# Preparing most weight tiles beside the first pair of blocks instead of beside the attention

## The chip, the cores and the metric

The kernel runs on one core of one Trainium2 chip. The metric is the device time of one execution in microseconds (us), given as the median of several runs. A core has TensorE (PE in the profile, with its weight loads as PEld), VectorE (DVE), ScalarE (ACT), GpSimd (POOL) and SyncE (SP), which here issues most of the DMAs.

## The reference

Attention inside chunks of 64 tokens, then two feed-forward layers: one with a squared ReLU (d_ff 2048) and one gated by SiLU (d_ff 1536). All of it is in float32.

```python
def _attn_ref(q, k, v):                      # q, k, v: (8, 8, 576, 64)
    scores = scale * np.matmul(q_c, k_c.transpose(0, 1, 2, 4, 3))   # chunks of 64 tokens
    scores = scores - np.max(scores, axis=-1, keepdims=True)
    attn = np.exp(scores)
    attn = attn / (np.sum(attn, axis=-1, keepdims=True) + 1e-09)
    out = np.matmul(attn, v_c)
...
def _moe_ref(x, w_in, w_out):                # x: 4608 x 512, w_in: 512 x 2048
    h = np.maximum(x @ w_in, 0.0)
    return (h * h @ w_out).astype(np.float32)
...
def _moe2_ref(x, w_gate, w_val, w_out):      # d_ff 1536
    g = x @ w_gate
    silu = g * (1.0 / (1.0 + np.exp(-g)))
    val = x @ w_val
    return (silu * val @ w_out).astype(np.float32)
```

## The kernel before

**Blocks and sets.** The 4608 tokens are nine blocks of 512. They are worked on in five sets: block 0 alone, then four pairs. Attention goes by units of 256 tokens, two in a block; `EARLY` is 6, so the opening has the units of blocks 0, 1 and 2, and the units of each later set are worked on beside the set before it.

**Products in parts.** Each matmul operand is split into a high part (`high`, ACT, L154) and a low part (`low`, DVE, L157), and a product is three matmuls of 128x512 (`three`, L464 to L466). For a pair of blocks a job (`Pair`) needs seven products of six matmuls, after a scheme that saves an eighth of the products; its seven operands are sums and differences of the blocks (`Operands.sums`, `make`). For block 0 a job (`Single`) has four such products, 24 matmuls. There is one job for each pair of f tiles and each set: `n1` is 8, the pairs are `keys1`. A job (n, m) is that of set n and pair m. Its methods `p15`, `p6`, `p27` are run in its own turn, while `p4` and `p3` are run in the turn of the job behind it (`Products.run`, `late`). `p15` copies the running sum `px` out on ACT (`kept`) between product 1 and product 6, `p6` does so before product 7.

**The preparation.** `prep_pair` makes the weight tile W of one pair of f tiles in seven steps: load of two raw tiles of 64-bit words (512 KB each), `decode1` (ACT, L129 and L130), `decode2` (DVE, then two additions on GpSimd, L139), `decode3` (DVE, L144) with the first casts, the first lows with four sums on DVE, the cast of the sums, and the last low, after which W is stored to DRAM where the pair is a moving one. Pairs 0, 3 and 6 stay in SBUF; the others (`moving1`) are stored and loaded again for each later set (`load_combo`, L230; `ask` starts the load two uses ahead).

**The opening.** It is one loop (L758), in which PE, ACT, DVE and GpSimd keep the order in which the code is written (`ordered`). SyncE's order is set by a planner. In iteration i unit i has its scores (`attn_products`, `attn_less_max`, `attn_exp`, `attn_normed`), unit i-1 is turned, and unit i-2 has its values and goes out; three steps of preparation i and three of preparation i-1 stand between them. From iteration 4 on the jobs of block 0 are given, three at once and then one in each iteration; job 7 follows after the first job of the first pair. The sums of the pair are made in iteration 8.

**The stages behind.** From L1020 on only PE keeps the written order; the other engines' orders are the planner's. A job of a pair has four quarters, at each of which `beside1` puts other work: the attention of the next set, its sums, its operands.

**Memory.** Tiles of 4 KB a partition (raws, m, s, q, k, v, e, p, z, x, all operands, g) share 31 buffers of the tag `big`. W has five buffers (`wp`). The scores and the values of the later units share one PSUM tile (`banks2`, tag `a`, one buffer); six banks (`psb`) serve the rest. A tile gets its buffer at its first write, in the order of the code, and gives it back when all that read it are done.

Of the kernel before, what the change touches and what calls it, by code (L numbers as in the profile page):

```python
# [28 lines left out]
def attention_mlp_mlp_kernel(  # L29
# [29 lines left out]
    nc = tc.nc  # L59
# [9 lines left out]
    upb = BLOCK // UNIT  # L69
# [12 lines left out]
    ident = const.tile([P, P], F32, name="ident")  # L82

    def duo(name, dtype=F32):
        return big.tile([P, 2, BLOCK], dtype, tag="big", name=name)
# [40 lines left out]
    def decode1(raws, m):  # L126

        for t, raw in enumerate(raws):
            nc.scalar.activation(out=m[:, t, :], in_=word(raw, 1, F32), func=AF.Abs)  # L129
            nc.scalar.activation(out=word(raw, 0, I32), in_=word(raw, 0, U32), func=AF.Copy, scale=2.0**-29)  # L130

    def decode2(raws, m):
        mi = m.bitcast(I32)
        nc.vector.tensor_scalar(out=m, in0=m, scalar1=LEAST, scalar2=MOST, op0=ALU.max, op1=ALU.min)
        nc.vector.tensor_scalar(
            out=mi, in0=mi, scalar1=5, scalar2=2, op0=ALU.logical_shift_left, op1=ALU.logical_shift_right
        )
        for t, raw in enumerate(raws):
            nc.gpsimd.tensor_tensor(out=mi[:, t, :], in0=mi[:, t, :], in1=word(raw, 0, I32), op=ALU.add)  # L139

    def decode3(raws, m):
        mi = m.bitcast(I32)
        for t, raw in enumerate(raws):
            nc.vector.scalar_tensor_tensor(  # L144
                out=mi[:, t, :],
                in0=word(raw, 1, I32),
                scalar=TOP,
                in1=mi[:, t, :],
                op0=ALU.bitwise_and,
                op1=ALU.bitwise_or,  # L150
            )

    def high(src, hi):
        nc.scalar.copy(out=hi, in_=src)  # L154
# [25 lines left out]
    combos = {}  # L180
    wdram = {}

    def new_combo():
        return wp.tile([P, 2, 7, half], F32R, tag="W", name="W")
# [7 lines left out]
    def prep_pair(key, raws, keep, store):  # L192

        pair = raws.take(2)
        yield
        m = duo("m")
        decode1(pair, m)
        yield
        decode2(pair, m)
        yield  # L200
        decode3(pair, m)
        w = new_combo()
        a1, a22 = m[:, 0, :].rearrange("p (i c) -> p i c", i=2), m[:, 1, half:]
        high(a1, w[:, 0, 0:2, :])
        high(a22, w[:, 0, 2, :])
        yield
        low(a1, w[:, 0, 0:2, :], w[:, 1, 0:2, :])
        low(a22, w[:, 0, 2, :], w[:, 1, 2, :])
        s = big.tile([P, 4, half], F32, tag="big", name="s")
        a11, a12, a21 = m[:, 0, :half], m[:, 0, half:], m[:, 1, :half]  # L210
        s1, s2, s3, s4 = (s[:, i, :] for i in range(4))
        tt = nc.vector.tensor_tensor
        tt(out=s1, in0=a21, in1=a22, op=ALU.add)
        tt(out=s2, in0=s1, in1=a11, op=ALU.subtract)
        tt(out=s3, in0=a11, in1=a21, op=ALU.subtract)
        tt(out=s4, in0=a12, in1=s2, op=ALU.subtract)
        yield
        high(s, w[:, 0, 3:7, :])
        yield
        low(s, w[:, 0, 3:7, :], w[:, 1, 3:7, :])  # L220
        if store:
            wdram[key] = combo_dram(key)
            nc.sync.dma_start(out=wdram[key], in_=flat(w))
        if keep:
            combos[key] = w
        yield
# [171 lines left out]
    def attn_turned(u):  # L398
        ts, pt = at[u], duo("p")
        for j in range(2):  # L400
            for c in range(2):
                part = slice(c * CH, (c + 1) * CH)
                nc.scalar.copy(out=pt[part, j, :], in_=ts[j ^ c][part, :])
        at[u] = pt
# [252 lines left out]
    work = Work()  # L657
    n1 = nf1 // 2

    keys1 = [("i", fp) for fp in range(n1)]  # L660
    keys2 = [(name, fp) for fp in range(n2) for name in "gv"]
    moving1 = set(keys1) - set(keys1[::3])
# [3 lines left out]
    def raws_of(keys, ahead):  # L666
        return Raws([sources[name][2 * fp + t] for name, fp in keys for t in range(2)], ahead)
# [56 lines left out]
            self.late()  # L724


    make_identity(nc, ident)
    raws1 = raws_of(keys1, 0)
    preps = [prep_pair(key, raws1, True, key in moving1) for key in keys1]
    up1 = Products(keys1, moving1, 2, 1, lambda key: squared)  # L730

    def x_sums(n):
        up1.ops[n] = Operands()
        up1.ops[n].sums([xraw.pop(b) for b in sets[n]])

    early = list(range(EARLY))
    ready = {"x": upb + 2, "pair": len(early) + 2}

    def prepare(f, steps=1):
        if 0 <= f < n1:
            for _ in range(steps):
                next(preps[f])

    def loads(i):
        if i < len(early):
            attn_qk(early[i])
        prepare(i)
        if 1 <= i <= len(early):  # L750
            attn_v(early[i - 1])

    with ordered(ET.PE, ET.Activation, ET.DVE, ET.Pool):
        make_identity(nc, ident)
        loads(0)
        loads(1)
        given = 0
        for i in range(n1 + 1):  # L758
            loads(i + 2)
            unit = early[i] if i < len(early) else None  # L760
            turned = early[i - 1] if 0 <= i - 1 < len(early) else None
            valued1 = early[i - 2] if 0 <= i - 2 < len(early) else None
            if unit is not None:
                attn_products(unit)
            if turned is not None:
                attn_turn_pe(turned)
            if valued1 is not None:
                attn_values(valued1)
            prepare(i)
            prepare(i - 1)  # L770
            if i == ready["x"]:
                x_sums(0)
                up1.ops[0].make(1, 2, 4)
            prepare(i - 1)
            if i == ready["pair"]:
                x_sums(1)
                up1.ops[1].make(1, 5)
            if turned is not None:
                attn_turned(turned)
            prepare(i)  # L780
            if unit is not None:
                attn_less_max(unit)
                attn_exp(unit)
            prepare(i - 1)
            if i == ready["pair"]:
                up1.ops[1].make(6, 2, 7)
            if unit is not None:
                attn_normed(unit)
            if valued1 is not None:
                attn_out(valued1)  # L790
            if i >= ready["x"]:
                while given < min(n1, i - 1):
                    up1.run(0, given)
                    given += 1
            prepare(i)

    class Down:

# [182 lines left out]
    def attention_step(n, t):  # L981

        if n < len(sets):
            units = [b * upb + x for b in sets[n] for x in range(upb)]
            for what in ("out", "turn", "scores", "qk"):
                for u, when in zip(units, WHEN[what]):
                    if when == t:
                        if what == "out":
                            attn_values(u)
                            attn_out(u)  # L990
                        elif what == "turn":
                            attn_v(u)
                            attn_turn(u)
                        elif what == "scores":
                            attn_scores(u)
                        else:
                            attn_qk(u)

    def beside1(n, m):
        def at_quarter(i):  # L1000
            t = 4 * m + i
            attention_step(n + 1, t)
            attention_step(n + 2, t - LAST)
            if n + 1 < len(sets):
                if t == 24:
                    x_sums(n + 1)
                if t - LAST in OPS:
                    up1.ops[n + 1].make(*OPS[t - LAST])
            else:
                if t % 2 == 0:  # L1010
                    work.step(1)
                if t == LAST - 8:
                    down1.begin()
                if t == LAST - 4:
                    down1.split(0)

        return at_quarter

    attention_step(2, -3)
    with ordered(ET.PE):  # L1020
        for n in range(1, len(sets)):
            if n + 1 == len(sets):
                raws = Raws(w_out, 2)
                for f in range(nf1):
                    work.add(prep_plain("o", f, raws))
            for m in range(n1):
                up1.run(n, m, beside1(n, m))
                if n == 1 and m == 0:
                    up1.run(0, n1 - 1)
        up1.finish()  # L1030
    combos.clear()

# [158 lines left out]
```

## Time and profile before

| | us |
|---|---|
| median of 3 runs | 1702.23 |
| lowest, highest | 1698.13, 1702.32 |
| the profiled execution, its own time | 1701.53 |
| its span in the trace | 1699.8 |
| PE busy | 1612.9 |
| DVE busy | 1023.0 |
| ACT busy | 817.4 |

The profile is of one execution. Its span goes from the first to the last instruction, and the execution's own time is 1.7 us longer. An engine's busy time leaves out waits and the issue of DMAs. Where a row tells what ended an idle time, the name behind the arrow is that of the instruction or the DMA that was waited for. The clock is the granted share of TensorE's full clock, 2.4 GHz.

### The profile page before, as it was taken

To read this page: it belongs to the slowest core of one execution; us is meant where nothing else is said; L and a number is where in the kernel's file an instruction comes from. 1 tells how busy PE (TensorE), PEld (TensorE's weight loads), DVE (VectorE), ACT (ScalarE), POOL (GpSimd) and SP (SyncE) were. 2 spreads that over 40 slices of the span, in tenths; PEclk is the share of its full clock that TensorE was granted. 3 is DMA by queue.
4 is the path that set the end of the run, shared out by engine and by line. 5 is a ranking of instruction groups with operands and counts; after the bars stand their busy time and mean duration, and the time that the engine had idled before them with its cause. 6 is when DMAs were issued, how large, how long until landed. Compare 5 with 4: busy or idle time off the path is not lost.

```text
span 1699.8 us, 23601 instructions
## 1 busy us (share of the span) xinstructions
PE 1612.9 (95%) x9408; PEld 1324.9 (78%) x9408; DVE 1023.0 (60%) x1268; ACT 817.4 (48%) x1165; POOL 130.9 (8%) x94
## 2 busy tenths in 40 slices
PE   3868999999999999999999999999998999999997
PEld 3756777778888888888888788788787788788886
DVE  7884464655467656562312646547448796787884
ACT  5774676768775444442212434334335553434441
POOL 3220001010122111110000000000000120000000
PEclk8888999999999999999999999999999999999999
DMA  8555887887976668784309685567568999563342
GB/s 335 211 217 209 278 282 260 289 282 257 349 240 247 246 250 292 283 305 133 116 37 369 230 297 204 198 242 244 192 250 297 343 377 409 200 198 111 105 144 50
DMA packets 140367, 407.10 MB, mean 240 GB/s; under 512 B 47840, under 2 KB 57056, under 8 KB 128736
## 3 DMA queue, kind: packets, MB, share of 16 engines
q1 hardware_dynamic: 129888, 367.83, 61.2%
q10 hardware_dynamic: 10368, 37.75, 5.8%
q8 instruction: 74, 1.21, 0.3%
q14 instruction: 37, 0.30, 0.1%
HBM read 278.92 MB, written 123.47 MB: 237 GB/s over the span
## 4 chain that ended last, share of the span: by engine, by line
PE 82%; DMA 6%; DVE 6%; ACT 2%; issue 2%; SPq 1%; POOL 1%; DVEq 0%; ACTq 0%; POOLq 0%
PE px L464 10%; PE px L466 10%; PE px L465 9%; PE acc L464 6%; PE acc L466 6%; PE acc L465 6%; PE py L464 5%; PE pz L466 5%; PE py L465 5%; PE py L466 5%; PE pz L465 5%; PE pz L464 5%; DMA k<-in_k_dram 4%; PE accs L464 2%; PE accs L466 2%; PE accs L465 2%
## 5 line engine op out<-in xcount | busy, mean ns | idle before, releaser
L464 PE MATMUL px<-hi,W 128*128 128x512 f32 x640 | 252.3, 394 | 9.0 <-ACT hi L154 5.5
L466 PE MATMUL px<-lo,W 128*128 128x512 f32 x640 | 250.4, 391 | 3.6 <-DVE lo L157 3.6
L465 PE MATMUL px<-hi,W 128*128 128x512 f32 x640 | 249.9, 391 | 0.0
L139 POOL TENSOR_TENSOR m<-m,raw 128x512 int32<-128x512 int32 x68 | 94.0, 1399 | 1005.4 <-ACT u L532 565.1
L532 ACT COPY u<-px 128x512 f32<-128x512 f32 x160 | 92.5, 578 | 150.4 <-PE px L466 150.3
L464 PE MATMUL acc<-hi,w 128*128 128x512 f32 x416 | 161.8, 389 | 0.0
L465 PE MATMUL acc<-hi,w 128*128 128x512 f32 x416 | 161.8, 389 | 0.0
L466 PE MATMUL acc<-lo,w 128*128 128x512 f32 x416 | 161.5, 389 | 0.0
L464 PEld LDWEIGHTS px<-hi,W 128*128 128x128 f32 x640 | 120.7, 189 | 38.1 <-ACT hi L154 6.3
L518 DVE TENSOR_TENSOR g<-pz,u 128x512 f32<-128x512 f32 x112 | 76.9, 687 | 115.3 <-PE pz L466 74.9
L466 PEld LDWEIGHTS px<-lo,W 128*128 128x128 f32 x640 | 120.7, 189 | 29.8 <-DVE lo L157 4.4
L633 DVE TENSOR_TENSOR g<-g,sig 128x1024 f32<-128x1024 f32 x54 | 65.9, 1220 | 125.7 <-ACT sig L632 125.6
L157 DVE TENSOR_TENSOR lo<-graw,hi 128x1024 fp32r<-128x1024 f32 x72 | 91.4, 1269 | 82.7 <-PE acc L465 42.8
L465 PEld LDWEIGHTS px<-hi,W 128*128 128x128 f32 x640 | 120.7, 189 | 24.4
L154 ACT CAST hi<-h 128x1024 fp32r<-128x1024 f32 x93 | 95.4, 1053 | 92.0 <-DVE h L885 21.9
L464 PE MATMUL pz<-hi,W 128*128 128x512 f32 x320 | 126.3, 395 | 8.3 <-ACT hi L154 8.3
L466 PE MATMUL pz<-lo,W 128*128 128x512 f32 x320 | 126.5, 395 | 3.1 <-DVE lo L157 3.1
L464 PE MATMUL py<-hi,W 128*128 128x512 f32 x320 | 128.1, 400 | 0.0
L465 PE MATMUL pz<-hi,W 128*128 128x512 f32 x320 | 126.1, 394 | 0.0
L465 PE MATMUL py<-hi,W 128*128 128x512 f32 x320 | 125.9, 394 | 0.0
L466 PE MATMUL py<-lo,W 128*128 128x512 f32 x320 | 125.9, 393 | 0.0
L157 DVE TENSOR_TENSOR lo<-h,hi 128x1024 fp32r<-128x1024 f32 x93 | 110.1, 1211 | 12.2 <-ACT hi L154 6.8
(123 smaller groups left out, 3116.0 us busy)
## 6 DMA issues: line engine op xcount, KB each, us to landing
W<-wv SPq DMA_DIRECT2D x30, 1792.0 KB, 8.6
g<-g ACTq DMA_DIRECT2D x72, 512.0 KB, 4.5
graw<-g SPq DMA_DIRECT2D x72, 512.0 KB, 4.2
W<-wi SPq DMA_DIRECT2D x20, 1792.0 KB, 9.1
W<-wg SPq DMA_DIRECT2D x20, 1792.0 KB, 8.3
h<-g SPq DMA_DIRECT2D x54, 512.0 KB, 8.3
h<-h SPq DMA_DIRECT2D x54, 512.0 KB, 6.3
raw<-in_w_out_dram SPq DMA_DIRECT2D x28, 512.0 KB, 7.7
```

Of the source, the lines that this page charges most:

```text
L139: nc.gpsimd.tensor_tensor(out=mi[:, t, :], in0=mi[:, t, :], in1=word(raw, 0, I32), op=ALU.add)
L154: nc.scalar.copy(out=hi, in_=src)
L157: nc.vector.tensor_tensor(out=lo, in0=src, in1=hi, op=ALU.subtract)
L464: nc.tensor.matmul(out=ps, lhsT=lh, rhs=rh, start=first, stop=False, skip_group_check=on)
L465: nc.tensor.matmul(out=ps, lhsT=ll, rhs=rh, start=False, stop=False, skip_group_check=on)
L466: nc.tensor.matmul(out=ps, lhsT=lh, rhs=rl, start=False, stop=last, skip_group_check=on)
L518: nc.vector.tensor_tensor(out=o, in0=ps, in1=r, op=ALU.add)
L532: nc.scalar.copy(out=r, in_=self.x)
L633: nc.vector.tensor_tensor(out=g[j], in0=g[j], in1=s, op=ALU.mult)
```

## The change

The opening no longer goes through eight preparations side by side, six steps in each iteration. All preparations are put into one queue (`work`), with two raw tiles loaded ahead, and one step is taken before the loop and three in each of its now eight iterations (`EARLY` + 2). Block 0's jobs are given one in an iteration, from iteration 4 on, and only if their tile is prepared. The sums and the first five operands of the first pair are made after the loop. In the first pair's stage each quarter of a job takes one more step of the queue; after each job of the pair but the first, one job of block 0 is run, with a step of the queue at each of its quarters, until block 0 has all eight. `since` goes from 1 to 2: the first pair uses the tiles as they were prepared, and the reloads begin with the second pair. One of the two calls of `make_identity` goes.

```diff
--- before.py
+++ after.py
@@ -724,10 +724,10 @@
             self.late()
 
 
-    make_identity(nc, ident)
-    raws1 = raws_of(keys1, 0)
-    preps = [prep_pair(key, raws1, True, key in moving1) for key in keys1]
-    up1 = Products(keys1, moving1, 2, 1, lambda key: squared)
+    raws1 = raws_of(keys1, 2)
+    for key in keys1:
+        work.add(prep_pair(key, raws1, True, key in moving1))
+    up1 = Products(keys1, moving1, 2, 2, lambda key: squared)
 
     def x_sums(n):
         up1.ops[n] = Operands()
@@ -735,27 +735,23 @@
 
 
 
+
     early = list(range(EARLY))
-    ready = {"x": upb + 2, "pair": len(early) + 2}
-
-    def prepare(f, steps=1):
-        if 0 <= f < n1:
-            for _ in range(steps):
-                next(preps[f])
+    ready = upb + 2
 
     def loads(i):
         if i < len(early):
             attn_qk(early[i])
-        prepare(i)
         if 1 <= i <= len(early):
             attn_v(early[i - 1])
 
     with ordered(ET.PE, ET.Activation, ET.DVE, ET.Pool):
         make_identity(nc, ident)
         loads(0)
+        work.step()
         loads(1)
         given = 0
-        for i in range(n1 + 1):
+        for i in range(len(early) + 2):
             loads(i + 2)
             unit = early[i] if i < len(early) else None
             turned = early[i - 1] if 0 <= i - 1 < len(early) else None
@@ -766,33 +762,27 @@
                 attn_turn_pe(turned)
             if valued1 is not None:
                 attn_values(valued1)
-            prepare(i)
-            prepare(i - 1)
-            if i == ready["x"]:
+            work.step()
+            if i == ready:
                 x_sums(0)
                 up1.ops[0].make(1, 2, 4)
-            prepare(i - 1)
-            if i == ready["pair"]:
-                x_sums(1)
-                up1.ops[1].make(1, 5)
-            if turned is not None:
-                attn_turned(turned)
-            prepare(i)
             if unit is not None:
                 attn_less_max(unit)
                 attn_exp(unit)
-            prepare(i - 1)
-            if i == ready["pair"]:
-                up1.ops[1].make(6, 2, 7)
+            if turned is not None:
+                attn_turned(turned)
+            work.step()
             if unit is not None:
                 attn_normed(unit)
             if valued1 is not None:
                 attn_out(valued1)
-            if i >= ready["x"]:
-                while given < min(n1, i - 1):
-                    up1.run(0, given)
-                    given += 1
-            prepare(i)
+            work.step()
+            if i >= ready and keys1[given] in combos:
+                up1.run(0, given)
+                given += 1
+        x_sums(1)
+        up1.ops[1].make(1, 5)
+        up1.ops[1].make(6, 2, 7)
 
     class Down:
 
@@ -999,6 +989,8 @@
     def beside1(n, m):
         def at_quarter(i):
             t = 4 * m + i
+            if n == 1:
+                work.step()
             attention_step(n + 1, t)
             attention_step(n + 2, t - LAST)
             if n + 1 < len(sets):
@@ -1025,8 +1017,9 @@
                     work.add(prep_plain("o", f, raws))
             for m in range(n1):
                 up1.run(n, m, beside1(n, m))
-                if n == 1 and m == 0:
-                    up1.run(0, n1 - 1)
+                if n == 1 and m > 0 and given < n1:
+                    up1.run(0, given, lambda i: work.step())
+                    given += 1
         up1.finish()
     combos.clear()
```

## Rows read from the trace of the kernel before

**Rows 1.** The page: PE's busy time and its digits in 40 slices.
```profile
PE 1612.9 (95%) x9408; PEld 1324.9 (78%) x9408; DVE 1023.0 (60%) x1268; ACT 817.4 (48%) x1165; POOL 130.9 (8%) x94
...
PE   3868999999999999999999999999998999999997
```

**Rows 2.** Windows: stretch, its us, busy PE, PEld, DVE, ACT, POOL, clock, DMA, GB/s.
```profile
0.00:60.00 60.00, 28.50 (x771) 26.91 (x772) 49.04 (x66) 35.94 (x60) 19.89 (x20) 0.77 0.90 342
60.00:112.80 52.80, 47.87 (x551) 39.91 (x549) 38.39 (x52) 40.82 (x72) 16.21 (x10) 0.97 0.44 169
112.80:161.00 48.20, 31.91 (x226) 24.23 (x225) 26.62 (x31) 22.82 (x29) 1.91 (x1) 0.82 0.56 198
161.00:227.30 66.30, 65.31 (x637) 53.15 (x638) 34.46 (x43) 46.86 (x73) 5.72 (x3) 1.00 0.79 277
...
59.30:75.90 16.60, 16.60 (x74) 13.56 (x72) 11.85 (x13) 10.91 (x18) 4.73 (x3) 0.99 0.38 132
131.30:138.10 6.80, 5.96 (x74) 5.01 (x75) 3.39 (x4) 1.34 (x2) 0.00 (x0) 0.50 0.75 277
```

**Rows 3.** Timeline of PE: start, us, instruction, [idle before and what ended it].
```profile
24.74 1.40 PE L340 MATMUL s<-k,q 64*64 64x64 f32 x64 [3.04 <-issue]
...
36.68 1.16 PE L340 MATMUL s<-k,q 64*64 64x64 f32 x64 [1.33 <-issue]
...
116.69 0.50 PE L464 MATMUL px<-hi,W 128*128 128x512 f32 x1 [3.85 <-ACT hi L154]
...
120.46 0.79 PE L466 MATMUL px<-lo,W 128*128 128x512 f32 x1 [3.04 <-DVE lo L157]
...
132.14 1.99 PE L340 MATMUL s<-k,q 64*64 64x64 f32 x64 [5.86 <-DMA k<-in_k_dram]
...
143.33 0.50 PE L464 MATMUL px<-hi,W 128*128 128x512 f32 x1 [1.62 <-ACT hi L154]
...
160.99 0.50 PE L464 MATMUL px<-hi,W 128*128 128x512 f32 x1 [1.38 <-DMA W<-wi]
```

**Rows 4.** Groups by shape, 20 to 60 us: count, busy us, mean ns, idle before.
```profile
L144 DVE SCALAR_TENSOR_TENSOR m<-raw,m 128x512 int32<-128x512 int32 x6 | 8.8, 1506 | 0.0
...
L139 POOL TENSOR_TENSOR m<-m,raw 128x512 int32<-128x512 int32 x6 | 7.6, 1280 | 13.3 <-ACT W L154 8.8 <-DMA q<-in_q_dram 4.5
...
L372 POOL TENSOR_TENSOR e<-e,rec 128x1024 f32<-128x1024 f32 x3 | 6.5, 2153 | 8.6 <-DVE rec L371 8.6
...
L129 ACT ACTIVATE m<-raw 128x512 f32<-128x512 f32 x7 | 4.6, 663 | 0.0
...
L360 DVE TENSOR_TENSOR e<-s,mx 128x1024 f32<-128x1024 f32 x3 | 3.7, 1224 | 0.1
...
L455 ACT COPY x<-xps 128x256 f32<-128x256 f32 x8 | 2.4, 386 | 0.0
...
L157 DVE TENSOR_TENSOR lo<-x,hi 128x1024 fp32r<-128x1024 f32 x2 | 2.4, 1222 | 0.1
...
L154 ACT CAST hi<-x 128x1024 fp32r<-128x1024 f32 x2 | 2.0, 1047 | 0.0
```

**Rows 5.** Timeline of SyncE, its DMA issues around unit 6's k.
```profile
122.74 0.32 SPq L223 DMA_DIRECT2D wi<-W  x1
123.16 0.39 SPq L324 DMA_DIRECT2D k<-in_k_dram  x1
```

**Rows 6.** The page's DMA issues: count, KB each, median us to landing.
```profile
g<-g ACTq DMA_DIRECT2D x72, 512.0 KB, 4.5
```

**Rows 7.** Groups by shape, 161 to 227.3 us, the first pair's stage.
```profile
L532 ACT COPY r<-px 128x512 f32<-128x512 f32 x6 | 3.6, 592 | 1.7 <-PE px L466 1.7
```

**Rows 8.** Waits of SyncE's queue, 30 to 230 us: total us, times, longest.
```profile
SPq L223 <- DVE W L157: 62.0, 5, 24.5
SPq L114 <- DVE lo L157: 9.4, 2, 8.6
SPq L329 <- DMA g<-g: 8.2, 1, 8.2
```

## Prediction

> **What bounds the kernel now.** I read the page first: TensorE (PE) is busy 95% of the span, and its digits fall below 8 only in the first four of forty slices [rows 1]. So PE sets the end and a change can only add or remove PE idle time or half-speed time; all products stay the same in number. Next the windows by stage: in the first 60 us PE is busy 28.5 and VectorE (DVE) 49.0; from 60 to 112.8 PE has 47.9 of 52.8; from 112.8 to 161 only 31.9 of 48.2, at a mean clock of 0.82; from 161 to 227.3, the stage of the first pair of blocks, 65.3 of 66.3, with DVE at 34.5 and ScalarE (ACT) at 46.9 [rows 2]. Then the timeline of PE for the waits: the score products of the units come every 11.9 us (24.74, 36.68), since one preparation and one attention unit share DVE; after the jobs of block 0 PE waits 3.85 and 3.04 us for the split operands of the pair, 5.86 us for the load of k of unit 6, 1.62 us for a split, and 1.38 us for a reloaded W [rows 3]. The opening thus costs far more than the steady stage, and it is there that the change works; the steady stage has next to nothing to give.
>
> **The opening, added up.** Before, an iteration has a whole preparation on DVE. After, it has three of seven steps. Of the 11.9 us, the two reductions and the subtraction of a unit take 3 x 1.22 = 3.7 (L360 and its like) [rows 4]; the remaining 8.3, times 3/7, is 3.5, so DVE needs about 7.2 us an iteration. It doesn't get down to that. I laid the written order of the four ordered engines end to end with the durations of [rows 4], each instruction starting when its engine and its inputs are free, with PE at half speed up to 60 us. For the kernel before, the first lo product of the pair comes out at 119.8, where the trace has 120.46 [rows 3], so the addition is good to a microsecond. After, scores start at 5.8, 13.6, 21.5, 32.0, 42.1 and 59.4: steps 3 and 4 of a preparation follow each other directly on DVE with two GpSimd additions (2 x 1.28) between them, so DVE stands still, and iteration 4 still has the split of block 0's operands. The last unit's values end at 83.3. Then there is a tail: ACT has four decodes of the fourth preparation (each 0.57 after the last) before the copies out of unit 5, which end at 87.9; the GpSimd additions end at 90.3, the last decode on DVE at 90.9; four sums of 1.15 follow, to 95.5, and the first lo at 96.7. PE does three jobs of block 0 in this time, not seven, and is idle from 83.3 to 92.3 and from 93.1 to 96.8. The pair starts 119.8 - 96.8 = 23.0 us sooner, but four jobs of 16.6 / 3 = 5.5 us (59.3 to 75.9 holds three) [rows 2] are now behind it: 22.1 us. **Gain 0.9 us** (from -2 to +3: the addition's own error twice). So what seems to be saved is only moved.
>
> **The waits just behind.** In the kernel before, k of unit 6 is issued at 123.16, behind a store of W at 122.74 in the same SyncE queue [rows 5], which is why PE waits 5.86. After, that store is gone from this place. The load needs buffers of the tag big that are handed out in the order of the code (below), so it follows the last split, at about 97; at 4.5 us for 512 KB [rows 6] S of unit 6 can start at 102.5, where PE is ready at 99.0: 3.5 instead of 5.86, **gain 2.4** (0 to 5.9). Reloads of W in the first pair's stage fall away, since the tiles are still there from their preparation: **gain 1.4** (the wait at 160.99) [rows 3]; five stores and five raw pairs use the same queue, spread over more time. The second identity on GpSimd goes; it ends before the first k lands and costs nothing either way.
>
> **The stage of the first pair.** Here stand the rest of preparation 4, four whole preparations and five jobs of block 0, 5 x 5.5 = 28 us of PE more. DVE gets about 4.4 x 8.3 = 37 us, against 31.8 free of 66.3 before and 28 more: it fits. ACT has 19.4 free and 28 more, and gets about 4.4 x 4.7 = 21 for the preparations (four decodes of 0.66, casts of 1.05 and, on three quarters as many columns, 1.0) and 5 x 2.3 = 12 for the jobs (two ReLU of 0.6, a square of 1.05): 33 of 47, so ACT is at some 85%. Where a pair's job follows a job of block 0, no product of the previous job stands between product 1 and product 6, nor between 6 and 7: six matmuls, 1.4 us, are all that hides a copy of px. A copy of 0.59 [rows 7] that comes behind one running instruction of 1.05 (the casts of L154) [rows 4] is 0.25 late; with two copies in each of five such jobs, **cost 2.5** (0 if ACT is always free, 5 if each comes behind two).
>
> **Buffers** are the heart of it. Tag big has 31. I counted, in the order of the code, the tiles between first write and last read. Before, the stage has 14 operands of the pair (hi and lo of seven), up to nine tiles of attention, up to four g, and block 0's six operands only through its first two jobs; not all of these at once, and 25 at most. After, block 0's six stay until its job 7, which comes after the pair's job 5, and each preparation holds two raws, two more ahead, m and s: the count passes 31 in jobs (1,1) to (1,3) and reaches 33, so some first write has to wait for a release. That such waits happen and what they take, the trace shows: a raw load waited 8.6 us for a lo (DVE) to free its source, a v load 8.2 us for the store of a g to land [rows 8]. After, the one that hurts is e (L360): while it waits, the scores stay in their PSUM tile; that tag has one buffer, which the values product needs too, and PE, in written order, stops before L439 with all jobs behind it. Units 8 and 9 are the ones whose e falls into jobs (1,2) and (1,3): **2 x 8.2 = 16.4** (none to four: 0 to 33). The price is taken at the v load's wait, since that too is a g store to land. After the 5.86 wait the clock was 0.50 for 6.8 us, with PE busy 5.96 of it (131.3 to 138.1) [rows 2]: half of that, 3.0, is lost. I count it after each: **2 x 3.0 = 6.0** (0 to 12). The half-speed time at the start of the pair I take as unchanged. W's five buffers: the tile of preparation 7 waits for the last use of tile 4, in the job after (1,4); its user comes a whole pair later, so no cost.
>
> **Sum.** -0.9 - 2.4 - 1.4 + 2.5 + 16.4 + 6.0 = +20.2. The profiled execution took 1701.5 (span 1699.8), 0.7 under the median of 1702.2; so 1721.7 for such an execution, 1722.4 against the median: **1722**.
>
> **A rule that speaks for the change.** The rows show the opening bound by DVE for 40 us and the stage behind by PE [rows 2]. The Trainium skill (Perfetto Trace Analysis, Optimization Strategy) says that a kernel in which the most-contended engine changes over time may gain by interleaving those regimes. By that the sum would be that of rival A. It speaks of engines, and DVE does have the room; the same page adds, for consistent bubbles, that a lack of SBUF for the next tile may be behind them, and no row of before shows one in this stage.
>
> **Rivals.** *A, the interleaving pays.* The mechanism is SyncE's queue: without the store ahead of k and without reloads nothing is late. Then 5.86 + 3.0 + 1.4 + 0.9 = 11.2 fall away: 1691. It decides where at every e of jobs (1,1) to (1,3) a buffer is free, for which preparations would have to run so far ahead that raws and s are gone; against it stands the count of 33. *B, buffers suffice but nothing is gained:* -0.9 - 2.4 - 1.4 + 2.5 and one half-speed stretch of 3.0 in the longer idle before the pair: 1703. For it: waits may fall on raws, which nothing needs at once. *C, SyncE becomes the bound.* W's stores wait for DVE at the head of that queue: 62.0 us in five, 12.4 each [rows 8], and behind them now stand the set-2 loads of q, k, v and the transposing copies that the values need. Three stores (4, 5, 7) in this stage: 37.2 in place of 16.4 + 6.0: 1737. Against it: DVE has room here, so a low is not long in coming. That the change doesn't do what it says can be left aside: 25 steps, seven a preparation, are three preparations and four steps, whatever the times.
>
> **How the numbers follow.** Forecast 0.60, A 0.13, B 0.15, C 0.12. The likeliest case runs from 1708 (one e wait without its clock) to 1740. The range reaches down to 1698, which takes in B, and up to 1740, which takes in C's centre; A and half of what is above C are left out, under 0.2. About 0.3%, 5 us, is what a measurement of this kernel can tell from no change: faster 0.13 (A), same 0.15 (B), slower 0.72.
>
> **What would show it.** The first px near 92, its first lo near 97, after three jobs of block 0 and nine us of idle PE: the opening's addition holds. PE waits of 6 to 9 us before L439 in jobs (1,2) and (1,3), with e of L360 late and a g store, a raw or an m released just before: the buffers. k of unit 6 waited for by 2 to 5 us: the queue. If instead PE is at 65 of 66 us through the alternating jobs, A or B holds and the count of buffers was no limit; if the waits end in transposing copies or v loads behind a store of W, C. A first lo past 100 or before 93 would mean that the opening was added up wrongly.

## The result and the profile after

The changed kernel takes **1719.07 us** (median, 1717.68 to 1720.44), against 1702.28 for the kernel before on the same chip: a ratio of **1.0097**, with an interval of 1.008 to 1.0114. It is 16.8 us slower; 1722 was forecast. The profiled execution has a span of 1716.9.

First the page: TensorE's busy time and its digits in 40 slices, to be laid beside [rows 1].

```profile
span 1716.9 us, 23606 instructions
...
PE 1615.0 (94%) x9408; PEld 1325.2 (77%) x9408; DVE 1023.1 (60%) x1268; ACT 817.7 (48%) x1165; POOL 128.2 (7%) x92
...
PE   4767799999999999999999999999999999999997
```

PE, DVE and ACT are busy as long as before, to within 0.2% (PE 2.1 us longer). The other 15.0 of the 17.1 us between the two spans are idle time, and it lies in the first five slices: the low digits now reach from the opening into the first pair's stage (the fifth slice is 172 to 215 us). So next the timeline of PE, with the longest idle times from the opening's end to the last job of this stage; columns as in [rows 3].

```profile
92.40 0.80 PE L464 MATMUL px<-hi,W 128*128 128x512 f32 x1 [9.62 <-ACT hi L154]
...
97.63 0.79 PE L466 MATMUL px<-lo,W 128*128 128x512 f32 x1 [4.01 <-DVE lo L157]
...
113.11 0.50 PE L464 MATMUL px<-hi,W 128*128 128x512 f32 x1 [2.08 <-ACT hi L154]
...
116.04 0.80 PE L466 MATMUL px<-lo,W 128*128 128x512 f32 x1 [2.17 <-DVE lo L157]
...
137.92 0.50 PE L464 MATMUL px<-hi,W 128*128 128x512 f32 x1 [0.96 <-ACT r L532]
...
154.29 2.10 PE L439 MATMUL xps<-p,v 64*64 64x64 f32 x64 [10.68 <-issue]
...
185.20 2.10 PE L439 MATMUL xps<-p,v 64*64 64x64 f32 x64 [10.98 <-issue]
```

The opening ends as it was added up: first product of the pair at 92.40, first lo at 97.63. Scores of unit 6 come with no wait, where [rows 3] has 5.86. Then PE stands still twice, 10.68 and 10.98 us, before values (L439) in the jobs (1,2) and (1,3). The values are those of units 6 and 7; the tile in PSUM that they need is held by the scores of units 8 and 9 (the expectations below call the waits by these two). "Issue" means that the row shows no releaser, so the reader has to turn to the engine that must empty the tile, VectorE. Its timeline from the maximum (L358) of unit 8's scores to the subtraction e (L360) that empties it:

```profile
140.73 1.23 DVE L358 TENSOR_REDUCE mx<-s 128x16 f32<-128x1024 f32 x1 [5.42 <-PE s L340]
141.98 0.69 DVE L134 TENSOR_SCALAR m<-m 128x1024 f32<-128x1024 f32 x1
142.71 0.69 DVE L135 TENSOR_SCALAR m<-m 128x1024 int32<-128x1024 int32 x1
144.85 2.35 DVE L144 SCALAR_TENSOR_TENSOR m<-raw,m 128x512 int32<-128x512 int32 x2 [1.44 <-POOL m L139]
149.90 0.69 DVE L157 TENSOR_TENSOR W<-m,W 128x512 fp32r<-128x512 f32 x1 [2.70 <-ACT W L154]
...
151.18 1.24 DVE L411 STREAM_TRANSPOSE z<-e 128x1024 f32<-128x1024 f32 x1
...
152.97 1.22 DVE L360 TENSOR_TENSOR e<-s,mx 128x1024 f32<-128x1024 f32 x1
```

The inputs of e are ready at 141.96, and e starts at 152.97, 11 us later, without a wait of its own: the planner has put it behind the last step that reads the raws of a preparation (L144) and behind what follows there. In the program e has the buffer of one of those raws. A missing buffer thus shows as order, not as a wait.

That preparation is late for a like reason. Its decode on ScalarE (L129, at 140.73) waits for the scores of unit 8 on PE, which it doesn't read: its m has the buffer of that unit's q. The second stop reads as the first does. The maximum of unit 9 is there at 172.57, and e follows 11.3 us later, directly behind the last reader (L216) of the m whose buffer it has:

```profile
171.34 1.23 DVE L358 TENSOR_REDUCE mx<-s 128x16 f32<-128x1024 f32 x1 [7.74 <-PE s L340]
...
183.41 0.43 DVE L216 TENSOR_TENSOR s<-m,s 128x256 f32<-128x256 f32 x1
183.87 1.23 DVE L360 TENSOR_TENSOR e<-s,mx 128x1024 f32<-128x1024 f32 x1
```

### The profile page after: what moved, and what is told of

It is laid out like the page before. It is cut to its first block, busy times and chain, and to the rows that moved or that the text cites. A ratio compares the mean times of both kernels' runs of the same rounds, so it can differ in the third digit from the quotient of the medians.

```text
span 1716.9 us, 23606 instructions
## 1 busy us (share of the span) xinstructions
PE 1615.0 (94%) x9408; PEld 1325.2 (77%) x9408; DVE 1023.1 (60%) x1268; ACT 817.7 (48%) x1165; POOL 128.2 (7%) x92
## 4 chain that ended last, share of the span: by engine, by line
PE 79%; DVE 5%; DMA 4%; issue 3%; ACT 3%; SPq 1%; POOL 0%; DVEq 0%; POOLq 0%; ACTq 0%
PE px L464 10%; PE px L466 9%; PE px L465 9%; PE acc L466 5%; PE acc L465 5%; PE acc L464 5%; PE pz L466 5%; PE py L464 4%; PE pz L464 4%; PE pz L465 4%; PE py L465 4%; PE py L466 4%; PE accs L466 2%; PE accs L465 2%; PE accs L464 2%
## 5 line engine op out<-in xcount | busy, mean ns | idle before, releaser
L532 ACT COPY u<-px 128x512 f32<-128x512 f32 x160 | 92.5, 578 | 159.5 <-PE px L466 159.5
L466 PEld LDWEIGHTS px<-lo,W 128*128 128x128 f32 x640 | 121.1, 189 | 32.8 <-DVE lo L157 7.4
L157 DVE TENSOR_TENSOR lo<-graw,hi 128x1024 fp32r<-128x1024 f32 x72 | 91.4, 1270 | 82.6 <-PE acc L465 42.8
L157 DVE TENSOR_TENSOR lo<-h,hi 128x1024 fp32r<-128x1024 f32 x93 | 110.4, 1216 | 12.2 <-ACT hi L154 6.8
```

What stands on the lines that cost most here:

```text
L157: nc.vector.tensor_tensor(out=lo, in0=src, in1=hi, op=ALU.subtract)
L466: nc.tensor.matmul(out=ps, lhsT=lh, rhs=rl, start=False, stop=last, skip_group_check=on)
L532: nc.scalar.copy(out=r, in_=self.x)
```

## The experiments

Two theories. **Theory 1**, the prediction's: 33 buffers of the tag `big` are wanted and 31 are there, so e stands behind a release. **Theory 2**, rival C: the stores of W in SyncE's queue and the raws behind them are late, and DVE's order with them. The times of all runs, each ratio against the kernel before on the same chip:

| kernel | us | ratio [interval] |
|---|---|---|
| after | 1719.07 | 1.0097 [1.008, 1.0114] |
| after, six buffers freed | 1699.71 | 0.9992 [0.9977, 1.0007] |
| after, no stores of W | 1721.55 | 1.0132 [1.0113, 1.0151] |
| after, 30 buffers | 1733.48 | 1.0193 [1.0169, 1.0217] |
| before, 28 buffers | 1706.3 | 1.0032 [1.0014, 1.0049] |
| after, no raws ahead | 1720.32 | 1.0103 [1.0074, 1.0132] |
| after, no raws ahead behind the opening | 1717.34 | 1.0099 [1.0077, 1.0122] |
| after, sums sooner | 1721.16 | 1.0106 [1.0069, 1.0144] |
| after, sums sooner, six buffers freed | 1706.07 | 1.0014 [1.0004, 1.0024] |
| before, sums sooner | 1705.94 | 1.0016 [0.9999, 1.0032] |
| before, sums sooner, q and k written sooner | 1703.26 | 1.0007 [0.9993, 1.0022] |
| before, q and k ahead of the store | 1696.87 | 0.9967 [0.9951, 0.9983] |
| before, both | 1699.02 | 0.9983 [0.997, 0.9996] |

**Six buffers freed.**

```diff
                 if n == 1 and m > 0 and given < n1:
+                    up1.ops[0] = up1.ops[1]
                     up1.run(0, given, lambda i: work.step())
```

> The kernel after, but the jobs of block 0 that stand between the pair's jobs take the pair's operands instead of block 0's own, so the six operand buffers of block 0 come free after its third job; count and shapes of all instructions stay. (Left out: those five jobs compute products of the pair's tokens.) Theory 1, shortage of buffers of the tag big: with six buffers more in the stage both idle times of 10.7 and 11.0 us before the values of units 8 and 9 go, and half-speed time with them: about 1695 to 1702. Theory 2, the stores of W and the late raw loads in SyncE's queue: nothing is taken from that queue, so 1719, with both idle times in place.

Measured 1699.71, 19.4 under the kernel after (about 18 by the two ratios), as theory 1 expected. The decode L129 in front of it now runs at 127.97 instead of 140.73, and DVE's timeline has e directly behind the maximum of unit 8:

```profile
142.88 1.22 DVE L358 TENSOR_REDUCE mx<-s 128x16 f32<-128x1024 f32 x1
144.13 1.22 DVE L360 TENSOR_TENSOR e<-s,mx 128x1024 f32<-128x1024 f32 x1
```

Both idle times are down to 0.44 and 0.71. SyncE's waits tell the same from the side of the loads (total us, times, longest; 97 to 200 us). The kernel after, all its rows of L329 and L114 over 2 us:

```profile
SPq L329 <- DMA g<-g: 19.4, 2, 10.6
SPq L329 <- DVE lo L157: 15.9, 1, 15.9
SPq L114 <- DMA g<-g: 10.6, 1, 10.6
...
SPq L329 <- DVE m L144: 7.8, 1, 7.8
...
SPq L114 <- DVE lo L157: 3.0, 1, 3.0
SPq L114 <- PE s L340: 2.1, 1, 2.1
```

A load waits there for a store of g to land or for the last reader of another tile: things that have nothing to do with it but a buffer. With six buffers freed one row of the two lines is left:

```profile
SPq L329 <- DVE s L213: 10.7, 1, 10.7
```

What the waits cost is read from the stretch between the pair's first product and the scores at the start of the next set, the same 1092 or 1093 matmul records in both kernels (columns as in [rows 2]). First after. This window ends with the last product, and the scores follow after the wait in the row below it, which is from the timeline of PE; so the stretch is 173.19 us:

```profile
92.40:264.66 172.26, 140.36 (x1092) 111.26 (x1092) 102.76 (x128) 104.34 (x153) 20.45 (x13) 0.89 0.52 186
...
265.59 1.16 PE L340 MATMUL s<-k,q 64*64 64x64 f32 x64 [0.93 <-PE pz L466]
```

Then with six buffers freed, up to the scores:

```profile
92.29:246.41 154.12, 137.40 (x1093) 108.81 (x1093) 105.79 (x129) 104.81 (x154) 22.10 (x13) 0.95 0.58 210
```

Of the 19.1 us between them, 32.8 - 16.7 = 16.1 are idle time and 140.4 - 137.4 = 3.0 are work at half speed. The two waits alone are 21.7 us; not all of it comes back, since in the kernel with free buffers PE waits 2.30 and 2.48 us for copies of r (L532), where after has 0.96 and 0.21, and 1.79 instead of 0.93 for k at the end of the stretch.

**No stores of W.**

```diff
-            wdram[key] = combo_dram(key)
-            nc.sync.dma_start(out=wdram[key], in_=flat(w))
+            if key[0] == "i" and key[1] > 2:
+                wdram[key] = wdram["i", 1]
+            else:
+                wdram[key] = combo_dram(key)
+                nc.sync.dma_start(out=wdram[key], in_=flat(w))
```

> The kernel after without the stores of the W tiles of pairs 4, 5 and 7; later sets load pair 1's stored tile in their place, so the loads stay in number and size. (Left out: those weights are wrong from the second pair of blocks on.) Theory 2 (SyncE): raws are then issued as soon as their buffers are free, ScalarE's decodes do not wait 3.8 and 1.8 us for them, and the idle times of 10.7 and 11.0 before the values shrink to 3 or less: 1697 to 1705. Theory 1 (buffers): raws need a free buffer, not a free queue, the idle times stay within 2 us of what they are: 1714 to 1719.

Measured 1721.55, no gain and 2.5 us above what theory 1 expected. The timeline of PE (L442 is L439 there, and the window cuts the first row short):

```profile
152.58 1.73 PE L442 MATMUL xps<-p,v 64*64 64x64 f32 x51 [9.29 <-issue]
...
183.88 2.10 PE L442 MATMUL xps<-p,v 64*64 64x64 f32 x64 [11.88 <-issue]
```

21.2 us in sum instead of 21.7. With no store in the queue the raws of the next preparation are issued at 134.15 instead of 135.78, and ScalarE's two waits for them are 3.1 us in sum instead of 5.6. That takes 1.4 us off the first wait of PE, and the second is 0.9 longer. Raw loads (L114) still wait 14.0 us for stores of g to land. Theory 2 falls as the cause of the two waits.

**30 buffers in the kernel after, 28 in the kernel before.** One number each in the line that makes the tag.

> The kernel after with 30 instead of 31 buffers of the tag big. Theory 1 (buffers): one fewer shifts further first writes behind releases, a third wait or longer ones: slower by 5 to 15 us, 1724 to 1734. Theory 2 (SyncE): no change, 1719 within 3.

> The kernel before with 28 instead of 31 buffers of the tag big. The count of the prediction gave at most 25 at once in the first pair's stage of this kernel: so 1702 within 3. If it is slower by more than 5, the kernel before already stands at the limit of its buffers and the count in the prediction is wrong.

One buffer fewer costs the changed kernel 14.4 us by the medians (8.6 between the two profiled spans), in the range that theory 1 gave. Its waits before the values are 8.94 and 12.74, no more than after's in sum, but copies and splits come late too (2.97, 1.95 and 1.66 for u and r, 1.39 for a lo), and the stretch of the windows above lasts 182.82 instead of 173.19, with PE busy 142.83. Three buffers fewer in the kernel before leave its first pair's stage untouched: the next set's scores start at 246.59, as against 246.78. So this stage wants no more than 28, which agrees with the count of 25. The whole kernel is 3.9 us slower, which is outside the 3 expected and short of the 5 that would have refuted the count. It arises behind this stage, and where was not followed up; the tag matters later too, which the prediction had not looked at.

**No raws ahead**, in the whole kernel (`raws_of(keys1, 0)`), then from iteration 6 of the opening on:

```diff
         for i in range(len(early) + 2):
+            if i == len(early):
+                raws1.ahead = 0
             loads(i + 2)
```

> The kernel after with no raw tiles loaded ahead in the preparations, so each preparation holds two buffers of the tag big fewer; the computation is that of the reference. Theory 1 (buffers, 33 wanted and 31 there): with two fewer wanted the waits before the values of units 8 and 9 lose at least half of their 21.7 us: 1700 to 1711, if ScalarE's decodes, whose raws now come later, do not hold the chain up in the opening (each raw pair then waits for its own load, some 4.5 us, in three preparations: up to 5 us of it could show at the first product of the pair, now at 92.4). Theory 2 (SyncE's queue): raws come later still, so the waits grow: 1719 to 1730.

> The kernel after with two raw tiles loaded ahead in the opening as before, and none from its iteration 6 on, so that only the preparations beside the first pair hold two buffers of the tag big fewer; the computation is that of the reference. Theory 1 (buffers): the first product of the pair stays at 92.4 (it came 3.4 us later where nothing was loaded ahead anywhere) and the waits before the values of units 8 and 9 shrink as they did there, from 10.7 and 11.0 to 5.5 and 8.0: 8.2 us less, 1709 to 1714. Theory 2 (SyncE and the decodes that wait for raws): raws come later, so the waits don't shrink: 1718 or more.

Both times that theory 1 expected were missed: 1720.32 and 1717.34; they lie at those of theory 2 (the second 0.7 under), whose waits should have grown or stayed, though. The waits did shrink, to 5.50 and 7.98 in the first (where the pair's first product came 3.4 us later, at 95.81), to these in the second:

```profile
137.91 0.50 PE L464 MATMUL px<-hi,W 128*128 128x512 f32 x1 [1.09 <-ACT r L532]
...
149.12 2.10 PE L439 MATMUL xps<-p,v 64*64 64x64 f32 x64 [5.46 <-issue]
...
166.17 0.50 PE L464 MATMUL px<-hi,W 128*128 128x512 f32 x1 [2.50 <-ACT r L532]
...
179.60 2.10 PE L439 MATMUL xps<-p,v 64*64 64x64 f32 x64 [6.22 <-issue]
```

That is 10.0 us less waiting for the values, but 3.0 more for three copies of r, counting 1.11 instead of 0.56 for the third, at 212. And work at half speed grew. Windows of PE's work behind the waits, first of this kernel (the middle one behind the copy of r), then of after:

```profile
149.00:154.20 5.20, 5.08 (x72) 4.37 (x73) 4.23 (x8) 2.97 (x5) 0.70 (x1) 0.52 0.55 184
166.00:171.90 5.90, 5.73 (x77) 4.63 (x78) 1.99 (x3) 2.52 (x5) 0.47 (x1) 0.71 0.72 237
179.00:185.20 6.20, 5.60 (x73) 4.79 (x74) 4.71 (x8) 3.60 (x7) 1.29 (x1) 0.54 0.27 66
```

```profile
154.00:158.00 4.00, 3.71 (x68) 3.33 (x69) 2.96 (x5) 1.99 (x2) 0.00 (x0) 0.50 0.66 200
185.00:188.90 3.90, 3.70 (x68) 3.33 (x69) 3.04 (x4) 1.78 (x3) 0.00 (x0) 0.52 0.31 71
```

After a wait of 10.7 us 3.7 us of work ran at half speed, after one of 5.5 us 5.1. From the pair's first product to the next set's scores this kernel takes 169.17 us with PE busy 143.29: 7.0 less idle than after's 173.19 and 2.9 more busy, so 4.0 in sum. Theory 1 stands in this (two buffers fewer wanted, 10 us less waiting); the step from waiting to time does not go one to one. The time itself doesn't show even the 4.0: the ratios are 1.0099 and 1.0097, and behind this point the profiled execution is 3.3 us longer than after's (1454.6 against 1451.3), for a reason that was not followed up.

One thing the count doesn't explain. Two fewer wanted are 31, as many as there are, and waits of 5.46 and 6.22 remain. So they don't begin where the count passes 31. A tile gets its buffer in the order of the code, and the tile that had it last may stand ahead in the code and yet have a reader that is late on its engine. Counted in the order of the code, 28 tiles are held where unit 8's e is written in the kernel after, and 30 at unit 9's: both get a buffer that is free by the code and not yet by the engines.

**The pair's sums sooner.** The prediction had put the tail of the opening down to decodes standing ahead of the pair's sums. So these were moved:

```diff
             if valued1 is not None:
                 attn_values(valued1)
+            if i == len(early) + 1:
+                attn_out(valued1)
+                x_sums(1)
+                up1.ops[1].make(1, 5)
             work.step()
```

(and taken away where they stood), in the kernel after, and there with the six buffers freed as well.

> The kernel after with the copies of unit 5, the sums of the first pair and its operands 1 and 5 put ahead of the last three preparation steps of the opening; nothing else. The prediction says that the opening loses its gain in its tail, because four decodes on ScalarE, two additions on GpSimd and the last decode on VectorE stand before these. Without them the last value ends at 82.8, copies take 3 and the sums 4.6 us: the first product of the pair at 87 to 89 instead of 92.4, its first lo at 91 to 93 instead of 97.6, so 4 to 6 us less, 1713 to 1715. If the three steps then delay the later stage by as much, 1719.

> The kernel after with both edits: the pair's sums ahead of the opening's last steps, and block 0's six buffers given back early. (Left out: as where those buffers alone were freed, five jobs of block 0 compute products of the pair's tokens.) With the sums moved alone the first lo of the pair came 4.3 us sooner, yet the values of unit 8 came at 154.19 as before it (154.29). Theory 1: those values hang on the release of buffers by a preparation, not on PE, so what PE gained was waited away; with the buffers freed the 4.3 us, less the 3.2 us that PE then waited for the next operand, remain: 1 to 4 us under the run with freed buffers alone, 1695 to 1699. If the gain is lost elsewhere (the preparations run later by the three steps): 1699.7 or more.

The gain expected of the first did not come, and in the second theory 1's account of that fell. In the first the first lo comes 4.3 us sooner, as the working said, and the kernel is no faster:

```profile
93.31 0.79 PE L466 MATMUL px<-lo,W 128*128 128x512 f32 x1 [2.28 <-DVE lo L157]
...
101.11 0.50 PE L464 MATMUL px<-hi,W 128*128 128x512 f32 x1 [3.17 <-ACT hi L154]
...
154.19 2.10 PE L439 MATMUL xps<-p,v 64*64 64x64 f32 x64 [10.71 <-issue]
```

The values come at 154.19, after's 154.29, as if the buffers had eaten the gain. But with the buffers freed as well it is 1706.07, 6.4 over the run with freed buffers alone (0.22%, or 3.7 us, by the two ratios, whose intervals just overlap). Its stretch from the first product on:

```profile
90.00:250.85 160.85, 142.06 (x1092) 111.41 (x1093) 108.81 (x133) 107.70 (x160) 24.65 (x15) 0.92 0.56 206
```

Against 154.12 and 137.40 above: 4.7 us more of half-speed work and 2.1 more idle, in return for a first product 2.3 us sooner: 4.4 us lost by the start of the next set. So the trace has the move costing by itself; that buffers had eaten its gain is not the explanation. The operands behind the first one now wait for the steps that the sums were put ahead of (3.41 us for a hi at 101.53), and more of the pair's work falls into the half-speed time.

**The same in the kernel before, and its k.** The same three lines moved there; then the loads of q and k of unit 6 written ahead of the opening's last preparation step; then these loads at the head of the last iteration, alone and with the sums:

```diff
         for i in range(n1 + 1):
+            if i == n1:
+                attn_qk(len(early))
             loads(i + 2)
```

> The kernel before with the same move alone: the first pair's sums and its operands 1 and 5 stand ahead of the steps of the last preparation in the loop's last iteration. The idle times of 3.85 and 3.04 us before the first product of the pair and its first lo go, in whole or most of it: 1695 to 1698. If the last preparation comes so late that the eighth job of block 0 waits for it: 1702.

> As the kernel before with the sums moved, and the loads of q and k of unit 6 written ahead of the last step of the opening's last preparation, so that they need not stand behind its store of W in SyncE's queue. If the wait of 5.86 us for k and the half-speed time behind it (3.0) go too: 1686 to 1690. If the planner of SyncE's order leaves the loads where they were, or they wait for their buffers: as with the sums alone, 1695 to 1698.

> The kernel before with the loads of q and k of unit 6 written ahead of the opening's last iteration, which puts both ahead of the last store of W in SyncE's queue; nothing else. This is what the changed kernel got for that wait, taken alone. If the 5.86 us wait for k hangs on that store: it goes, and with it the half-speed time behind it (3.0): 1693 to 1697. If the loads wait for a free buffer of the tag big instead: k lands no earlier, 1702.

> The kernel before with both: the pair's sums ahead of the steps of the last preparation, and q and k of unit 6 loaded ahead of the store of W. With the sums moved alone PE reached the first lo of the pair 1.9 us sooner and then waited 9.0 instead of 5.86 us for k. With k there in time both gains stand: 1690 to 1694. If the loads wait for buffers: 1702 to 1706.

The sums alone missed: 1705.94. The first lo comes at 118.57 instead of 120.46, and k then holds PE for 9.01 instead of 5.86 us, since the store ahead of it belongs to the preparation that the sums delay: the store is issued at 124.42 and k at 125.32, where [rows 5] has 122.74 and 123.16, and k takes 10.5 us to land instead of 8.8 (the window cuts the second row short):

```profile
118.57 0.79 PE L466 MATMUL px<-lo,W 128*128 128x512 f32 x1 [3.76 <-DVE lo L157]
...
135.99 0.38 PE L340 MATMUL s<-k,q 64*64 64x64 f32 x3 [9.01 <-DMA k<-in_k_dram]
```

Writing the loads a little sooner missed as well, with 1703.26, and changed nothing in SyncE's order: the store is issued at 124.76, q at 125.17, k at 125.65. At the head of the iteration it did. SyncE's timeline of the run with these loads alone:

```profile
95.99 0.39 SPq L324 DMA_DIRECT2D q<-in_q_dram  x1
96.43 0.95 SPq L324 DMA_DIRECT2D k<-in_k_dram  x1
108.17 0.34 SPq L230 DMA_DIRECT2D W<-wi  x1
123.46 0.34 SPq L223 DMA_DIRECT2D wi<-W  x1
```

Scores of unit 6 start at 127.54 with no wait (132.14 before), and the kernel takes 1696.87, as expected: 5.8 us by the medians or 0.33% under the kernel before (0.17 to 0.49%). It is the fastest kernel here and beats both: what the change gains at k, without the rest of the change. The half-speed time was expected to go with the wait and did not. From 82 us to the next set's scores (244.26, before 246.78) PE is 4.5 us less idle and 2.0 longer busy, so the trace shows where 2.5 us of the gain lie and not the rest. With the sums moved as well it is 1699.02, in neither of the ranges expected; the intervals don't separate the two, but the sums add nothing here either.

## Why the prediction was right

Step by step, by the terms of its sum; the measured ones are of the profiled executions, up to the scores at the start of the next set (246.78 before, 265.59 after: 18.8 us).

| term | forecast | measured |
|---|---|---|
| opening, with four jobs put behind it | -0.9 | -0.7 |
| k of unit 6 | -2.4 | -5.9 |
| reload of W | -1.4 | -1.4 |
| copies of px | +2.5 | +1.7 |
| fourth operand of the pair | none | +2.1 |
| two waits for e | +16.4 | +21.7 |
| half speed | +6.0 | +2.3 |
| sum | +20.2 | +19.8 |

*Opening.* First lo at 97.63 where 96.7 was added up; 120.46 - 97.63 = 22.8 us sooner, less the same four jobs of 22.1. The run with six buffers freed, 1699.71, is rival B's case (1703 was its price): without the waits for e nothing is gained in sum either. The working had PE at half speed up to 60 us, where the mean clock was 0.77 [rows 2]; its end came out within a microsecond all the same.

*k.* It was taken to be issued after the last split, at 97, and to be there at 102.5, 3.5 us late (97 and the 4.5 of [rows 6] make 101.5). It was issued at 97.61 and took 5.1 us to land, but PE was not ready at 99.0 as worked out: it ran at half speed from 97 to 103.5, and the scores came at 104.19, when k was there. So the whole 5.86 went, the upper bound of the 0 to 5.9 given.

*W and copies.* No wait for a reloaded W in this stage. The three waits for r are 0.96, 0.21 and 0.56. In the run with freed buffers they are 2.30, 2.48 and 0.55, 5.3 in sum, a little over the upper bound of 5: where nothing else is late, the copies are.

*The fourth operand* was left out. Its hi and lo wait 2.08 and 2.17 us, against 1.62 and 0.53 before:

```profile
144.59 0.50 PE L466 MATMUL px<-lo,W 128*128 128x512 f32 x1 [0.53 <-DVE lo L157]
```

Most of it is the lo. The subtraction that makes it (L157, 128x1024) took 2.90 us from 113.09 on, beside a multiplication of GpSimd (L372) from 113.00 to 114.90; in the kernel before the same subtraction took 1.23 us (143.31), with GpSimd idle. That the one comes from the other is not shown. Where the 0.46 at hi come from was not followed up.

*The waits for e* came in the two jobs named, (1,2) and (1,3), and from the cause named: freeing six buffers takes them away, one buffer fewer makes the stage longer still. Off was their size, 10.7 and 11.0 instead of 8.2 each, and what released the buffer: not the store of a g, which is what its price was taken from, but the last reader of a raw and of an m, with the decode steps of a preparation in between. Rival A asked for a free buffer at every e; in the run that has them it gains nothing that can be measured, so A's 1691 falls for another reason too: the copies of r and the fourth operand (5.3 + 2.1) take what k and W give (5.9 + 1.4).

*Half speed.* Measured is half of PE's busy time in the half-speed windows: 17.9 us of work in four of them in the kernel after (97.0 to 188.9), 13.4 in three before (one is in [rows 2]), so 2.3 more are lost, not 6.0. The half-speed time behind k, 3.0, went away with that wait, and behind a wait for e only 3.7 us of work ran slowly, not 6.0. So the errors cancel: the waits for e, the fourth operand and the opening came 7.6 us dearer than forecast, and k, the copies and the half speed 8.0 cheaper. That the two sums lie within 0.4 us is luck; the direction, the place and the cause are not.

The terms measured add up to 1.0 more than the 18.8 between the two starts; a wait of 0.99 for k at 181.26 in the kernel before, which the kernel after doesn't have, makes it up. Behind the start the kernel after is 1.7 us shorter in these executions, which was not followed up; the medians differ by 16.8.

*The rule that speaks for the change.* The run with freed buffers is the fair test of it: DVE's work does spread over the regime of PE, without loss, and without gain. By the Trainium skill (Perfetto Trace Analysis, Optimization Strategy), performance may be improved by interleaving regimes; this trace shows 0.9992 [0.9977, 1.0007] for that. That section of the Trainium skill also remarks that repeated gaps on the engine that should be saturated can mean too little SBUF for the next tile; the trace agrees, with two gaps of 10.7 and 11.0 us, gone with six buffers more.

## What to carry over

Before work is moved under a stage that is already full, count the buffers at its fullest point, with everything that the move keeps alive longer: here a count of 33 on 31 buffers came with two stops of 11 us, on an engine that does not use the missing buffer itself. Leave a margin, too: with a count of 31 on 31, stops of 5.5 and 6.2 us remained. A gap marked "issue" on the bound engine is to be followed to the instruction that empties the tile it needs, and from there to what stands ahead of that in its engine's order. And look for the part of a change that gains alone: here the place of two loads ahead of one store gave 0.33% without moving a preparation.

## What the runs showed that was not expected

A wait's price is not its length. Windows of the kernel after around the first wait (columns as in [rows 2]):

```profile
143.60:147.80 4.20, 0.01 (x1) 0.00 (x0) 2.35 (x2) 0.67 (x1) 2.45 (x2) 1.00 0.84 297
147.80:158.00 10.20, 3.71 (x68) 3.33 (x69) 7.06 (x11) 4.98 (x7) 0.00 (x0) 0.50 0.43 128
```

PE was idle and the granted clock still full, 2.4 GHz, in the first; in the second it was 1.2 GHz, at first with PE idle and then over 3.71 us of work. In the kernel with fewer raws ahead PE resumed after 5.46 us, and 5.08 us of its work ran at 0.52. So the wait of 10.7 us cost some 10.7 + 1.9, that of 5.5 us 5.5 + 2.5: of 5.2 us less waiting 4.6 remained. Estimates of a gain from a shortened wait should take the half-speed work behind it from rows, not in proportion.
